# Decode attention on one core: K, V and weights in 8 MB transfers of 64 KB runs, two ring slots at a time

## The chip, the core and the metric

The kernel runs on one core of a Trainium2 chip. The metric is the device time of one execution in microseconds (us); most executions of one kernel agree within 0.3%. All runs told here are of the fast, undisturbed state. A ratio is the mean time of one kernel's fast runs over the mean of the other kernel's fast runs of the same rounds, so it is not quite the ratio of the medians that are quoted.

PE is the matmul engine, VectorE (DVE), ScalarE (ACT) and GpSimd (POOL) are the other compute engines, and SP issues the large DMA transfers. MB in names of transfers means 4,194,304 bytes for "4 MB".

## The reference, cut to what matters

```python
# A: attention of one new token per sequence against a cache; B=4, H=32 heads, Sk=8192, Dh=128, bf16
q = (x @ wq) ...
scores = einsum("bhqd,bhkd->bhqk", q, k_cache) * Dh**-0.5
o = einsum("bhqk,bhkd->bhqd", softmax(scores), v_cache)
a = o @ wo
# B: a gated feed-forward, D=1024, F=3584:  b = x + silu(x@w_gate)*(x@w_up) @ w_down * sigmoid(x@w_r)
return g * a + (1 - g) * b            # g = sigmoid(sum(x * gate_w))
```

K and V are 537 MB together and the weights 39 MB, and each byte is used once. The kernel is therefore a stream: what matters is that the DMA engines never rest.

## The kernel before

A ring of five slots, 32 KB per partition (4 MB) each, holds what has arrived. A "piece" of K or V is two heads, 64 partitions each, so a partition receives one contiguous run of 32 KB. K is transposed on VectorE in four chunks and multiplied on PE; V is multiplied on PE against the probabilities. Eight K pieces make a group, which ends with a softmax over 16 heads. V follows eight pieces behind K.

```python
ring = tile_pool(name="ring", bufs=5)
def slot():
    return ring.tile([P, RING], BF, name="piece", tag="piece")     # 4 MB
...
def k_piece(u):
    ...
    kn = slot()
    nc.sync.dma_start(out=kn[:], in_=kv_view(A_k_cache, u))
    for c in range(JR // CJ):                                      # 4 chunks
        T = ttp.tile([P, CJ, 2, 32, 2], BF, name="T", tag="T")     # two buffers
        nc.vector.transpose(out=T..., in_=kn[:, c * CJ * Dh:(c + 1) * CJ * Dh]...)
        ... 8 matmuls into S_ps
        if c == 0:
            flush()                                                # finish() of the group before
    if t == GT - 1:
        softmax(g)
def softmax(g):
    ... max, all-reduce, exp (ACT) ...
    nc.vector.transpose(out=PT..., in_=PTs[:])
    nc.scalar.copy(out=Bv[0:W, :, :, 0, :], in_=Pv[0:W])
    nc.gpsimd.tensor_copy(out=Bv[W:P, :, :, 1, :], in_=Pv[W:P])
    ... rex (DVE), tot = all-reduce of rex (POOL)
    nc.vector.reciprocal(out=rinv[:], in_=tot[:])
def v_piece(u):
    ...
    nc.sync.dma_start(...)                                         # the last piece in four parts
    ... 32 matmuls into o_ps
    # every fourth piece: evict o_ps
    nc.scalar.activation(out=o_sb[:], in_=o_ps[:, 0, :], func=ACT.Copy, scale=mE[:, 0:1])
    nc.vector.scalar_tensor_tensor(out=o_sb[:], in0=o_ps[:, 1, :], scalar=mE[:, 1:2], in1=o_sb[:], ...)
```

## Time and profile before

| | before |
|---|---|
| median time | 1349.41 us (1349.13 to 1349.46) |
| bytes read | 575.68 MB, 427 GB/s over the span of 1347.8 us |
| PE, VectorE busy | 79%, 47% |
| first to last large packet (packet records) | 1341.5 us |
| from the last large packet to the end | 4.5 us |

The page of the kernel before: engines' busy time, the rate in 40 equal slices of the span, the main DMA queue (packets, MB, share of 16 engines' span), and two groups of transfers (size, and median us from issue to landing).

```profile
PE 1059.3 (79%) x4600; PEld 233.2 (17%) x2412; DVE 631.4 (47%) x375; ACT 41.5 (3%) x46; POOL 47.9 (4%) x115
...
GB/s 403 433 433 422 433 430 430 432 433 430 430 433 430 430 431 434 429 431 432 433 428 432 433 430 430 433 431 429 432 434 429 428 433 434 429 428 434 432 423 323
...
q1 hardware_dynamic: 22104, 575.68, 99.5%
...
piece<-in_A_k_cache_dram SPq DMA_DIRECT2D x64, 4096.0 KB, 39.4
piece<-in_A_v_cache_dram SPq DMA_DIRECT2D x63, 4096.0 KB, 39.1
```

The queue is busy for 99.5% of the span, and between the first and the last slice the rate never falls under 422 GB/s. The last two lines: a transfer lands 39 us after its issue, although 4 MB move in 9.7 us (4.194 MB at 431 GB/s). So about four transfers are queued at most times.

Now the place where compute is slowest, the end of a group (timeline of before: start, duration, engine, line, operation, and in brackets the idle time before and what ended it).

```profile
628.76 0.59 PE L401 MATMUL o_ps<-piece,PB 128*16 128x512 bf16 x2
...
629.40 0.69 ACT L411 ACTIVATE OS<-o_ps,mE 128x512 f32<-128x512 f32 x1 [74.68 <-PE o_ps L401]
630.12 0.75 DVE L412 SCALAR_TENSOR_TENSOR OS<-o_ps,mE,OS 128x512 f32<-128x512 f32 x1 [6.23 <-ACT OS L411]
...
632.48 1.25 DVE L367 STREAM_TRANSPOSE PT<-PTs 128x1024 bf16<-128x1024 bf16 x1 [1.33 <-ACT PTs L365]
...
633.87 1.88 POOL L373 COPY PB<-PT 64x1024 bf16<-64x1024 bf16 x1 [3.86 <-DVE rex L375]
...
636.33 0.25 DVE L379 RECIPROCAL rinv<-tot 128x16 f32<-128x16 f32 x1 [2.48 <-POOL tot L377]
636.50 4.44 DVE L336 STREAM_TRANSPOSE T<-piece 128x2048 uint32<-128x2048 uint32 x2
638.90 3.57 PE L342 MATMUL S_ps<-T,Z 128*128 128x512 bf16 x8 [9.54 <-DVE T L336]
...
647.44 2.31 DVE L336 STREAM_TRANSPOSE T<-piece 128x2048 uint32<-128x2048 uint32 x1 [2.50 <-PE S_ps L342]
```

The scheduler has put the eviction (L412) ahead of the rest of the softmax on VectorE, so everything behind it waits for the V matmuls that end at 629.4 us. The next group's transposes start only at 636.5 us. PE, idle for 9.5 us, then works at half clock (the granted clock is 0.50 from 635 to 645 us): 8 matmuls take 3.57 us, elsewhere 1.90. The first four transposes of the group end at 649.8 us. All this lateness costs nothing: the slices that hold this stretch (the 19th and 20th, each 33.7 us) show 432 and 433 GB/s.

### The profile page before, as it was taken

What the parts mean: (1) busy time and instruction counts of PE and PEld (TensorE: products, weight loads), DVE (VectorE), ACT (ScalarE), POOL (GpSimd) and SP (SyncE); (2) the same over time, 40 slices, a digit from 0 to 9 for tenths busy, and PEclk for the clock granted to TensorE, in tenths of its full rate; (3) what the DMA queues carried; (4) which work ended last, traced back from release to release, by engine and by line L of the source; (5) the groups of instructions that cost most, each with busy time, mean ns of one, the idle gap of its engine ahead of it and who ended that gap; (6) DMA issues with size and microseconds to landing.
All of it is one profiled execution on the core that took longest, in us unless ns stands there. A gap on an engine that the chain in (4) does not pass through costs nothing.

```text
span 1347.8 us, 8253 instructions
## 1 busy us (share of the span) xinstructions
PE 1059.3 (79%) x4600; PEld 233.2 (17%) x2412; DVE 631.4 (47%) x375; ACT 41.5 (3%) x46; POOL 47.9 (4%) x115
## 2 busy tenths in 40 slices
PE   2667779876978868876998769888788859797878
PEld 0111111211111111111212111211112112121111
DVE  3555755535544554454545454444544456346000
ACT  0000010001000010001000010000000010000000
POOL 2000000000000000000000000000000000000000
PEclk8878989898989989989898879899888979999899
DMA  9999999999999999999999999999999999999997
GB/s 403 433 433 422 433 430 430 432 433 430 430 433 430 430 431 434 429 431 432 433 428 432 433 430 430 433 431 429 432 434 429 428 433 434 429 428 434 432 423 323
DMA packets 22162, 576.22 MB, mean 428 GB/s; under 512 B 2399, under 2 KB 2407, under 8 KB 2925
## 3 DMA queue, kind: packets, MB, share of 16 engines
q1 hardware_dynamic: 22104, 575.68, 99.5%
q8 instruction: 27, 0.44, 0.1%
q14 instruction: 11, 0.08, 0.0%
q10 hardware_dynamic: 20, 0.02, 0.0%
HBM read 575.68 MB, written 0.01 MB: 427 GB/s over the span
## 4 chain that ended last, share of the span: by engine, by line
DMA 50%; PE 30%; DVE 11%; issue 6%; ACT 1%; POOL 1%; SPq 0%; DVEq 0%; ACTq 0%
DMA piece<-in_A_k_cache_dram 40%; PE o_ps L401 16%; PE S_ps L342 13%; DVE T L336 10%; DMA piece<-in_A_v_cache_dram 9%; PE small L419 1%; DMA piece<-in_A_wo_dram 1%; POOL PB L373 1%; DVE PT L367 1%; ACT PTs L365 1%; ACT OS L411 1%; DVE OS L412 1%; POOL tot L377 0%; PE acc L188 0%; PE o_ps L225 0%
## 5 line engine op out<-in xcount | busy, mean ns | idle before, releaser
L336 DVE STREAM_TRANSPOSE T<-piece 128x2048 uint32<-128x2048 uint32 x256 | 576.1, 2288 | 437.0 <-DMA piece<-in_A_k_cache_dram 321.1
L342 PE MATMUL S_ps<-T,Z 128*128 128x512 bf16 x2048 | 544.6, 416 | 246.6 <-DVE T L336 235.3
L401 PE MATMUL o_ps<-piece,PB 128*16 128x512 bf16 x2048 | 457.6, 382 | 14.8 <-DMA piece<-in_A_v_cache_dram 14.8
L342 PEld LDWEIGHTS <-Z 128*128 128x128 bf16 x1024 | 108.0, 105 | 667.2 <-issue 664.3
L401 PEld LDWEIGHTS <-PB 128*16 128x16 bf16 x1024 | 91.9, 90 | 373.1 <-issue 361.3
L412 DVE SCALAR_TENSOR_TENSOR OS<-o_ps,mE,OS 128x512 f32<-128x512 f32 x16 | 12.0, 751 | 174.6 <-ACT OS L411 174.6
L326 POOL TENSOR_TENSOR Z<-qa,mq 128x16 bf16<-128x16 bf16 x64 | 16.7, 262 | 1072.3 <-PE S_ps L342 1054.3
L411 ACT ACTIVATE OS<-o_ps,mE 128x512 f32<-128x512 f32 x16 | 11.0, 687 | 1040.5 <-PE o_ps L401 1040.5
L419 PEld LDWEIGHTS small<-selg,OS 128*128 128x128 f32 x128 | 24.9, 273 | 12.2 <-issue 11.1
L419 PE MATMUL small<-selg,OS 128*128 128x8 f32 x128 | 22.3, 302 | 0.0
L353 DVE TENSOR_REDUCE m<-S_ps 128x1 f32<-128x1024 f32 x8 | 9.8, 1225 | 15.9 <-PE S_ps L342 15.9
L188 PE MATMUL acc<-piece,LT 128*4 128x512 bf16 x64 | 14.9, 378 | 1.7 <-DMA piece<-in_A_wo_dram 1.6
L373 POOL COPY PB<-PT 64x1024 bf16<-64x1024 bf16 x8 | 15.1, 1884 | 29.1 <-DVE rex L375 29.1
L372 ACT COPY PB<-PT 64x1024 bf16<-64x1024 bf16 x8 | 15.3, 1908 | 10.6 <-DVE PT L367 10.6
L367 DVE STREAM_TRANSPOSE PT<-PTs 128x1024 bf16<-128x1024 bf16 x8 | 10.0, 1245 | 11.9 <-ACT PTs L365 11.9
L188 PE MATMUL acc<-piece,hT 128*4 128x512 bf16 x56 | 12.4, 379 | 0.0
L131 PE MATMUL small<-identb,x 6*128 6x6 bf16 x8 | 0.6, 194 | 14.2 <-DVE identb L128 14.2
L379 DVE RECIPROCAL rinv<-tot 128x16 f32<-128x16 f32 x8 | 2.0, 253 | 19.9 <-POOL tot L377 19.9
L365 ACT ACTIVATE PTs<-S_ps,negm 128x1024 bf16<-128x1024 f32 x8 | 8.9, 1113 | 70.0 <-DVE negm L362 70.0
L225 PE MATMUL S_ps<-piece,xw 128*4 128x512 bf16 x64 | 6.6, 591 | 3.0 <-DMA piece<-in_A_wq_dram 3.0
L422 DVE SCALAR_TENSOR_TENSOR OT<-small,sgb,rinv 128x8 bf16<-128x8 f32 x16 | 3.2, 202 | 11.7 <-PE small L419 11.7
L358 POOL PARTITION_ALL_REDUCE gmx<-mex x8 | 3.1, 390 | 81.9 <-issue 50.3
(72 smaller groups left out, 74.6 us busy)
## 6 DMA issues: line engine op xcount, KB each, us to landing
piece<-in_A_k_cache_dram SPq DMA_DIRECT2D x64, 4096.0 KB, 39.4
piece<-in_A_v_cache_dram SPq DMA_DIRECT2D x63, 4096.0 KB, 39.1
piece<-in_A_wq_dram SPq DMA_DIRECT2D x2, 4096.0 KB, 22.1
piece<-in_B_w_gate_dram SPq DMA_DIRECT2D x2, 3584.0 KB, 40.1
piece<-in_B_w_up_dram SPq DMA_DIRECT2D x2, 3584.0 KB, 34.6
piece<-in_A_wo_dram SPq DMA_DIRECT2D x6, 1024.0 KB
piece<-in_B_w_down_dram SPq DMA_DIRECT2D x1, 4096.0 KB, 35.6
piece<-in_A_v_cache_dram SPq DMA_DIRECT2D x4, 1024.0 KB, 32.6
```

Source lines behind the costliest of these rows:

```text
L188: nc.tensor.matmul(out_ap, lhsT=lhsT, rhs=rhs, start=start, stop=True, skip_group_check=True)
L326: nc.gpsimd.tensor_tensor(out=Z[:, :, 31:31 + P].rearrange("p e (s d c) -> p e s d c", s=HT, d=QH)[:, :, :, :, 0], in0=qa[:, :, h0:h0 + HT ...
L336: nc.vector.transpose(out=T[:].rearrange("p j h i e -> p (j h i e)").bitcast(U32), in_=kn[:, c * CJ * Dh:(c + 1) * CJ * Dh].bitcast(U32))
L342: nc.tensor.matmul(sps[:, z, :], lhsT=Z[:, he, s:s + P], rhs=T[:, 16 * z:16 * z + 16, half, :, e], start=(t == 0 and c == 0 and he == 0), ...
L365: nc.scalar.activation(out=PTs[:], in_=sps[:].rearrange("p z n -> p (z n)"), func=ACT.Exp, bias=negm[:, 0:1], scale=scale, accum_out=rs[:, ...
L367: nc.vector.transpose(out=PT[:].rearrange("p j i -> p (j i)"), in_=PTs[:])
L372: nc.scalar.copy(out=Bv[0:W, :, :, 0, :], in_=Pv[0:W])
L373: nc.gpsimd.tensor_copy(out=Bv[W:P, :, :, 1, :], in_=Pv[W:P])
L401: nc.tensor.matmul(o_ps[row:row + NM, e, :], lhsT=B_[:, JT * t + c, z, w].rearrange("p e s j -> p (e s j)"), rhs=vn[:, j0 * Dh:(j0 + 4) * ...
L411: nc.scalar.activation(out=o_sb[:], in_=o_ps[:, 0, :], func=ACT.Copy, scale=mE[:, 0:1])
L412: nc.vector.scalar_tensor_tensor(out=o_sb[:], in0=o_ps[:, 1, :], scalar=mE[:, 1:2], in1=o_sb[:], op0=ALU.mult, op1=ALU.add)
L419: nc.tensor.matmul(oT[:, :], lhsT=o_sb[:, q * Dh:(q + 1) * Dh], rhs=selg[:, q].rearrange("p t s -> p (t s)"), start=(q == 0), stop=(q == 3))
```

## The change

The intent is fewer, larger packets. A "pair" is four heads, 32 partitions (one quadrant) each, 8 MB in one transfer, with a contiguous run of 64 KB per partition over two neighbouring slots. With five slots every fifth pair wraps around and comes as two 4 MB transfers. The weights travel the same way, all but `wo`, whose transfers stay at 1 MB and less. A group is now four pairs and has one eviction instead of two.

```diff
-    ring = ctx.enter_context(tc.tile_pool(name="ring", bufs=5))
+    ring = const.tile([P, NS, RING], BF, name="ring")              # NS = 5
+    flat = ring[:].rearrange("p s n -> p (s n)")
+    def load_pair(src, n):
+        a = slots(2)
+        if a + 1 < NS:
+            lo = a * RING
+            nc.sync.dma_start(out=flat[:, lo:lo + 2 * n], in_=src)
+            return [flat[:, lo:lo + n], flat[:, lo + n:lo + 2 * n]]
+        halves = [ring[:, a], ring[:, 0]]
+        for i, half in enumerate(halves):
+            nc.sync.dma_start(out=half[:, 0:n], in_=src[:, i * n:(i + 1) * n])
+        return halves
...
-        return cache[b, h0:h0 + HT].rearrange("h (r j) d -> (h r) (j d)", j=JR)
+        return cache[b, h0:h0 + NQ].rearrange("h (r j) d -> (h r) (j d)", j=2 * JR)
...
-        nc.scalar.copy(out=Bv[0:W, :, :, 0, :], in_=Pv[0:W])
-        nc.gpsimd.tensor_copy(out=Bv[W:P, :, :, 1, :], in_=Pv[W:P])
+        for q in range(NQ):                       # quadrants 0, 2 on ACT; 1, 3 on POOL
+            ...
...
-        cut = 4 if u == NT - 1 else 1
+        if d < ND - 1:
+            vs = load_pair(vv, RING)
+        else:                                     # the last pair: 4 MB, then 4 x 1 MB
+            ...
```

More of the change, by code (lines that the diff above doesn't have):

```diff
@@ L69 @@
     DT = D // P
-    HT = 2
-    JR = Sk * HT // P
-    JC = JR // 16
-    GT = 8
-    JT = JC // 2
-    RT = 4
-    GH = GT * HT
-    RH = RT * HT
     NQ = 4
-    QH = NQ // HT
+    QP = P // NQ
+    JR = Sk // QP // 2
     CJ = 32
-    NT = Bn * H // HT
-    LAG = GT
+    JT = JR // CJ
+    RD = 2 * JT
+    GD = QP // RD
+    GH = GD * NQ
+    ND = Bn * H // NQ
+    LAG = GD
     FR = 4
@@ L87 @@
     RING = JR * Dh
+    NS = 5
     assert Sq == 1 and Dh == P and D % P == 0 and F % (P * FR) == 0
-    assert H == 32 and JR == 128 and JT * GT == 32 and GT % RT == 0 and H % GH == 0 and D % NB == 0
+    assert H % GH == 0 and JR == 128 and RD * GD == QP and D % NB == 0
     scale = float(Dh) ** -0.5
@@ L103, with slots @@
     nc.at_finalize(keep_weights)
+    ring = const.tile([P, NS, RING], BF, name="ring")
+    turn = [0]
+    def slots(n):
+        at = turn[0]
+        turn[0] = (at + n) % NS
+        return at
+    flat = ring[:].rearrange("p s n -> p (s n)")
[9 more added lines that the diff above has]
+        return halves
     def small(shape, dtype=F32):
         return mps.tile(shape, dtype, name="small", tag="small")
-    def slot():
-        return ring.tile([P, RING], BF, name="piece", tag="piece")
     NX = Bn + 2
@@ L134 @@
     xT = [xw[:, t, 0:Bn] for t in range(DT)]
-    R = const.tile([P, 4, P], BF)
+    R = ptp.tile([P, 4, P], BF, name="R", tag="PTs")
     nc.gpsimd.memset(R[:], 0.0)
@@ L140, with band @@
                                 base=-(64 * half + e), pattern=[[0, 4], [-2, 32]], channel_multiplier=1)
-    m32 = const.tile([P, GT, NQ], F32)
-    nc.gpsimd.memset(m32[:], 1.0)
-    nc.gpsimd.affine_select(out=m32[:], in_=m32[:], compare_op=ALU.is_ge, fill=0.0,
-                            base=0, pattern=[[-JT, GT], [-32, NQ]], channel_multiplier=1)
-    nc.gpsimd.affine_select(out=m32[:], in_=m32[:], compare_op=ALU.is_ge, fill=0.0,
-                            base=JT - 1, pattern=[[JT, GT], [32, NQ]], channel_multiplier=-1)
-    mask8 = const.tile([P, GH], F32)
-    nc.vector.tensor_reduce(out=mask8[:], in_=m32[:].rearrange("p t (s q) -> p (t s) q", q=QH), axis=AX.X, op=ALU.add)
-    pen8 = const.tile([P, GH], F32)
-    nc.vector.tensor_scalar(out=pen8[:], in0=mask8[:], scalar1=-1.0, scalar2=3.0e38, op0=ALU.add, op1=ALU.mult)
-    nmask8 = const.tile([P, GH], F32)
-    nc.vector.tensor_scalar(out=nmask8[:], in0=mask8[:], scalar1=-scale, scalar2=None, op0=ALU.mult)
-    selg = const.tile([P, 4, RT, HT], F32)
+    def band(t, width, steps):
+        nc.gpsimd.memset(t[:], 1.0)
+        nc.gpsimd.affine_select(out=t[:], in_=t[:], compare_op=ALU.is_ge, fill=0.0, base=0,
+                                pattern=[[-s, n] for s, n in steps], channel_multiplier=1)
+        nc.gpsimd.affine_select(out=t[:], in_=t[:], compare_op=ALU.is_ge, fill=0.0, base=width - 1,
+                                pattern=[[s, n] for s, n in steps], channel_multiplier=-1)
+    mask3 = const.tile([P, GD, NQ], F32)
+    band(mask3, RD, [(RD, GD), (QP, NQ)])
+    mask = mask3[:].rearrange("p t q -> p (t q)")
+    pen = const.tile([P, GH], F32)
+    nc.vector.tensor_scalar(out=pen[:], in0=mask, scalar1=-1.0, scalar2=3.0e38, op0=ALU.add, op1=ALU.mult)
+    nmask = const.tile([P, GH], F32)
+    nc.vector.tensor_scalar(out=nmask[:], in0=mask, scalar1=-scale, scalar2=None, op0=ALU.mult)
+    selg = const.tile([P, 4, GD, NQ], F32)
     nc.gpsimd.memset(selg[:], 0.0)
@@ L156 @@
         nc.gpsimd.affine_select(out=selg[:], in_=selg[:], compare_op=ALU.not_equal, fill=1.0,
-                                base=-8 * e, pattern=[[-1, 4], [-32, RT], [-4, HT]], channel_multiplier=1)
+                                base=-16 * e, pattern=[[-1, 4], [-32, GD], [-4, NQ]], channel_multiplier=1)
     mE4 = const.tile([P, 2, 4], F32)
-    nc.gpsimd.memset(mE4[:], 1.0)
-    nc.gpsimd.affine_select(out=mE4[:], in_=mE4[:], compare_op=ALU.is_ge, fill=0.0,
-                            base=0, pattern=[[-8, 2], [-32, 4]], channel_multiplier=1)
-    nc.gpsimd.affine_select(out=mE4[:], in_=mE4[:], compare_op=ALU.is_ge, fill=0.0,
-                            base=7, pattern=[[8, 2], [32, 4]], channel_multiplier=-1)
+    band(mE4, 16, [(16, 2), (32, 4)])
     mE = const.tile([P, 2], F32)
@@ L166 @@
     mq = const.tile([P, 1, NQ], BF)
-    nc.gpsimd.memset(mq[:], 1.0)
-    nc.gpsimd.affine_select(out=mq[:], in_=mq[:], compare_op=ALU.is_ge, fill=0.0,
-                            base=0, pattern=[[0, 1], [-32, NQ]], channel_multiplier=1)
-    nc.gpsimd.affine_select(out=mq[:], in_=mq[:], compare_op=ALU.is_ge, fill=0.0,
-                            base=31, pattern=[[0, 1], [32, NQ]], channel_multiplier=-1)
-    ZW = 31 + P + 1
+    band(mq, QP, [(0, 1), (QP, NQ)])
+    ZW = QP - 1 + P + 1
     Zt = [const.tile([P, 4, ZW], BF, name=f"Z{i}") for i in range(2)]
-    PB = [const.tile([P, 32, 2, 2, 2, HT, 4], BF, name=f"PB{i}") for i in range(2)]
+    PB = [const.tile([P, QP, 2, 2, 2, NQ, 4], BF, name=f"PB{i}") for i in range(2)]
     for z in Zt + PB:
@@ L209, in add_x, with x_rows, wq_piece @@
             mm_acc(acc[:, n * NB:(n + 1) * NB], dg[:], xf[:, n * NB:(n + 1) * NB])
-    wqv = A_wq.rearrange("(c t) n -> c t n", t=DT)
-    wgv = B_w_gate.rearrange("(c t) f -> c t f", t=DT)
-    wuv = B_w_up.rearrange("(c t) f -> c t f", t=DT)
-    wdv = B_w_down.rearrange("(g f r) n -> f g r n", f=P, r=FR)
+    TW = DT // 2
+    wdv = B_w_down.rearrange("(f i) n -> f (i n)", f=P)
     wov = A_wo.rearrange("(g p r) n -> p g r n", p=P, r=FR)
-    TW = 4
-    def x_rows(ps, w, t0, nb):
-        for t in range(TW):
-            for k in range(4):
-                for z in range((nb - k + 3) // 4):
-                    i = 4 * z + k
-                    nc.tensor.matmul(ps[32 * k:32 * k + Bn, z, :], lhsT=xT[t0 + t], rhs=w[:, t, i * NB:(i + 1) * NB],
-                                     start=(t0 + t == 0), stop=(t0 + t == DT - 1), skip_group_check=True)
-    def wq_piece(t0):
-        w = slot()[:, :TW * H * Dh].rearrange("p (t n) -> p t n", t=TW)
-        nc.sync.dma_start(out=w, in_=wqv[:, t0:t0 + TW, :])
-        x_rows(q_ps, w, t0, H * Dh // NB)
+    def x_rows(ps, ws, nb, cols):
+        for half, w in enumerate(ws):
+            for t in range(TW):
+                for k in range(4):
+                    for z in range((nb - k + 3) // 4):
+                        nc.tensor.matmul(ps[32 * k:32 * k + Bn, z, :], lhsT=xT[TW * half + t], rhs=cols(w, t, 4 * z + k),
+                                         start=(half + t == 0), stop=(half == 1 and t == TW - 1), skip_group_check=True)
+    def wq_piece():
+        N = H * Dh
+        ws = load_pair(A_wq.rearrange("(c t) n -> c (t n)", t=DT), TW * N)
+        x_rows(q_ps, ws, N // NB, lambda w, t, i: w[:, t * N + i * NB:t * N + (i + 1) * NB])
     def q_done():
@@ L246, in q_done, with gu_piece, cols @@
         nc.vector.tensor_copy(out=qa[:].rearrange("p e h b -> p e (h b)"), in_=qa_ps[:])
-    def gu_piece(view, w_i, t0):
-        w = slot()[:, :TW * F].rearrange("p (t n) -> p t n", t=TW)
-        nc.sync.dma_start(out=w, in_=view[:, t0:t0 + TW, :])
-        x_rows((o_ps, acc4)[w_i], w, t0, FG)
+    def gu_piece(view, w_i):
+        ws = load_pair(view.rearrange("(c t) f -> c (t f)", t=DT), TW * F)
+        def cols(w, t, i):
+            row = w[:, t * F:(t + 1) * F].rearrange("p (f i r) -> p f i r", i=FG, r=FR)
+            return row[:, :, i, :]
+        x_rows((o_ps, acc4)[w_i], ws, FG, cols)
     def h_done():
@@ L264, in h_done, with wd_piece @@
                                         in1=c12[:, 1:2, :].to_broadcast([P, kn, Bn]), op=ALU.mult)
-    def wd_piece(g0, ng):
-        w = slot()[:, :ng * FR * D].rearrange("p (g r n) -> p g r n", g=ng, r=FR)
-        nc.sync.dma_start(out=w.rearrange("p g r n -> p g (r n)"),
-                          in_=wdv[:, g0:g0 + ng].rearrange("f g r n -> f g (r n)"))
-        for g in range(ng):
-            for r in range(FR):
-                for n in range(NH):
-                    mm_acc(acc[:, n * NB:(n + 1) * NB], hT[:, g0 + g, r, :], w[:, g, r, n * NB:(n + 1) * NB],
-                           start=(g0 + g + r == 0))
+    def wd_piece():
+        NR = FG * FR // 2
+        ws = load_pair(wdv, NR * D)
+        for i in range(FG * FR):
+            w = ws[i // NR]
+            for n in range(NH):
+                at = (i % NR) * D + n * NB
+                mm_acc(acc[:, n * NB:(n + 1) * NB], hT[:, i // FR, i % FR, :], w[:, at:at + NB], start=(i == 0))
     WB = P * FR // Dh
@@ L294, in wo_block @@
         if home not in wo_home:
-            wo_home[home] = slot().rearrange("p (g r n) -> p g r n", g=4, r=FR)
+            wo_home[home] = ring[:, slots(1)].rearrange("p (g r n) -> p g r n", g=4, r=FR)
         w = wo_home[home][:, at]
@@ L313, in flush, with heads, kv_view, k_pair @@
             pending.pop(0)()
-    def heads(u):
-        return divmod(u * HT, H)
-    def kv_view(cache, u):
-        b, h0 = heads(u)
-        return cache[b, h0:h0 + HT].rearrange("h (r j) d -> (h r) (j d)", j=JR)
-    def k_piece(u):
-        b, h0 = heads(u)
-        g, t = divmod(u, GT)
-        Z = Zt[u % 2]
-        nc.gpsimd.tensor_tensor(out=Z[:, :, 31:31 + P].rearrange("p e (s d c) -> p e s d c", s=HT, d=QH)[:, :, :, :, 0],
-                                in0=qa[:, :, h0:h0 + HT, b:b + 1].to_broadcast([P, 4, HT, QH]),
-                                in1=mq[:].rearrange("p o (s d) -> p o s d", s=HT).to_broadcast([P, 4, HT, QH]), op=ALU.mult)
+    def heads(d):
+        return divmod(d * NQ, H)
+    def kv_view(cache, d):
+        b, h0 = heads(d)
+        return cache[b, h0:h0 + NQ].rearrange("h (r j) d -> (h r) (j d)", j=2 * JR)
+    def k_pair(d):
+        b, h0 = heads(d)
+        g, t = divmod(d, GD)
+        Z = Zt[d % 2]
+        nc.gpsimd.tensor_tensor(out=Z[:, :, QP - 1:QP - 1 + P].rearrange("p e (q c) -> p e q c", c=QP)[:, :, :, 0],
+                                in0=qa[:, :, h0:h0 + NQ, b], in1=mq[:].to_broadcast([P, 4, NQ]), op=ALU.mult)
         if t == 0:
@@ L331, in k_piece @@
         sps = S_ps[g]
-        kn = slot()
-        nc.sync.dma_start(out=kn[:], in_=kv_view(A_k_cache, u))
-        for c in range(JR // CJ):
+        ks = load_pair(kv_view(A_k_cache, d), RING)
+        for n in range(RD):
+            kn, c = ks[n // JT], n % JT
             T = ttp.tile([P, CJ, 2, 32, 2], BF, name="T", tag="T")
@@ L337, in k_piece @@
                                 in_=kn[:, c * CJ * Dh:(c + 1) * CJ * Dh].bitcast(U32))
-            s = 31 - (JT * t + c)
+            s = QP - 1 - (RD * t + n)
             for he in range(4):
@@ L342, in k_piece @@
                     nc.tensor.matmul(sps[:, z, :], lhsT=Z[:, he, s:s + P], rhs=T[:, 16 * z:16 * z + 16, half, :, e],
-                                     start=(t == 0 and c == 0 and he == 0),
-                                     stop=(t == GT - 1 and c == JT - 1 and he == 3))
-            if c == 0:
+                                     start=(t == 0 and n == 0 and he == 0),
+                                     stop=(t == GD - 1 and n == RD - 1 and he == 3))
+            if n == 0:
                 flush()
-        if t == GT - 1:
+        if t == GD - 1:
             softmax(g)
@@ L354, in softmax @@
         mex = stat.tile([P, GH], F32, tag="mex")
-        nc.vector.scalar_tensor_tensor(out=mex[:], in0=mask8[:], scalar=m1[:, 0:1], in1=pen8[:],
+        nc.vector.scalar_tensor_tensor(out=mex[:], in0=mask, scalar=m1[:, 0:1], in1=pen[:],
                                        op0=ALU.mult, op1=ALU.add)
@@ L359, in softmax @@
         gmm = stat.tile([P, GH], F32, tag="gmm")
-        nc.vector.tensor_tensor(out=gmm[:], in0=gmx[:], in1=nmask8[:], op=ALU.mult)
+        nc.vector.tensor_tensor(out=gmm[:], in0=gmx[:], in1=nmask[:], op=ALU.mult)
         negm = stat.tile([P, 1], F32, tag="negm")
         nc.vector.tensor_reduce(out=negm[:], in_=gmm[:], axis=AX.X, op=ALU.add)
-        PTs = ptp.tile([P, 1024], BF, name="PTs")
+        PTs = ptp.tile([P, 1024], BF, name="PTs", tag="PTs")
         rs = stat.tile([P, 1], F32, tag="rs")
@@ L368, in softmax @@
         B_ = PB[g % 2]
-        W = P // HT
         Pv = PT[:].rearrange("p (q j) i -> p i q j", j=4)
         Bv = B_[:].rearrange("p i z w e s j -> p i (z w e) s j")
-        nc.scalar.copy(out=Bv[0:W, :, :, 0, :], in_=Pv[0:W])
-        nc.gpsimd.tensor_copy(out=Bv[W:P, :, :, 1, :], in_=Pv[W:P])
+        for q in range(NQ):
+            at = slice(QP * q, QP * (q + 1))
+            if q % 2 == 0:
+                nc.scalar.copy(out=Bv[at, :, :, q, :], in_=Pv[at])
+            else:
+                nc.gpsimd.tensor_copy(out=Bv[at, :, :, q, :], in_=Pv[at])
         rex = stat.tile([P, GH], F32, tag="rex")
-        nc.vector.tensor_scalar(out=rex[:], in0=mask8[:], scalar1=rs[:, 0:1], scalar2=None, op0=ALU.mult)
+        nc.vector.tensor_scalar(out=rex[:], in0=mask, scalar1=rs[:, 0:1], scalar2=None, op0=ALU.mult)
         tot = stat.tile([P, GH], F32, tag="tot")
@@ L380, in softmax, with v_pair @@
         rinv_t[g] = rinv
-    NM = 8 * HT
-    def v_piece(u):
-        b, h0 = heads(u)
-        g, t = divmod(u, GT)
-        row = 32 * (t % RT)
-        B_ = PB[g % 2]
-        vn = slot()
-        vv = kv_view(A_v_cache, u)
-        cut = 4 if u == NT - 1 else 1
-        for c in range(cut):
-            lo, hi = c * RING // cut, (c + 1) * RING // cut
-            nc.sync.dma_start(out=vn[:, lo:hi], in_=vv[:, lo:hi])
+    NM = 8 * NQ
+    def v_pair(d):
+        b, h0 = heads(d)
+        g, t = divmod(d, GD)
+        row = NM * t
+        B_ = PB[g % 2]
+        vv = kv_view(A_v_cache, d)
+        if d < ND - 1:
+            vs = load_pair(vv, RING)
+        else:
+            vs = [ring[:, slots(1)] for _ in range(2)]
+            nc.sync.dma_start(out=vs[0], in_=vv[:, 0:RING])
+            for c in range(4):
+                lo, hi = c * RING // 4, (c + 1) * RING // 4
+                nc.sync.dma_start(out=vs[1][:, lo:hi], in_=vv[:, RING + lo:RING + hi])
         n = 0
-        for c in range(JT):
+        for c in range(RD):
+            vn = vs[c // JT]
             for z in range(2):
@@ L399, in v_piece @@
                     for e in range(2):
-                        j0 = 32 * c + 16 * z + 8 * w + 4 * e
+                        j0 = CJ * (c % JT) + 16 * z + 8 * w + 4 * e
                         nc.tensor.matmul(o_ps[row:row + NM, e, :],
-                                         lhsT=B_[:, JT * t + c, z, w].rearrange("p e s j -> p (e s j)"),
-                                         rhs=vn[:, j0 * Dh:(j0 + 4) * Dh], start=(n == 0), stop=(n == JR // 8 - 1),
+                                         lhsT=B_[:, RD * t + c, z, w].rearrange("p e s j -> p (e s j)"),
+                                         rhs=vn[:, j0 * Dh:(j0 + 4) * Dh], start=(n == 0), stop=(n == 4 * RD - 1),
                                          skip_group_check=True)
@@ L407, in v_piece @@
                         flush()
-        if t % RT < RT - 1:
+        if t < GD - 1:
             return
@@ L413, in v_piece @@
                                        op0=ALU.mult, op1=ALU.add)
-        r0 = RH * (t // RT)
         def finish():
-            oT = small([P, RH])
+            oT = small([P, GH])
             for q in range(4):
@@ L420, in finish @@
                                  rhs=selg[:, q].rearrange("p t s -> p (t s)"), start=(q == 0), stop=(q == 3))
-            hg = h0 + HT - RH
-            nc.vector.scalar_tensor_tensor(out=OT[:, hg:hg + RH, b], in0=oT[:, :], scalar=sgb[:, 1, b:b + 1],
-                                           in1=rinv_t[g][:, r0:r0 + RH], op0=ALU.mult, op1=ALU.mult)
+            hg = h0 + NQ - GH
+            nc.vector.scalar_tensor_tensor(out=OT[:, hg:hg + GH, b], in0=oT[:, :], scalar=sgb[:, 1, b:b + 1],
+                                           in1=rinv_t[g][:], op0=ALU.mult, op1=ALU.mult)
         pending.append(finish)
     gates()
-    wq_piece(0)
-    wq_piece(TW)
+    wq_piece()
     q_done()
-    side = [lambda: gu_piece(wgv, 0, 0), lambda: gu_piece(wgv, 0, TW), lambda: gu_piece(wuv, 1, 0),
-            lambda: (gu_piece(wuv, 1, TW), h_done()), lambda: wd_piece(0, 4), lambda: wd_piece(4, FG - 4)]
-    GE = NWB - RH // WB
+    gu_piece(B_w_gate, 0)
+    side = {1: lambda: (gu_piece(B_w_up, 1), h_done()), GD - 1: wd_piece}
+    GE = NWB - GH // WB
     order = []
-    for u in range(NT - 2):
-        order += [("k", u)] + [("v", u - LAG)] * (u >= LAG)
-    order += [("k", NT - 2), ("k", NT - 1)] + [("v", u) for u in range(NT - 2 - LAG, NT)]
-    for kind, u in order:
+    for d in range(ND):
+        order += [("k", d)] + [("v", d - LAG)] * (d >= LAG)
+    order += [("v", d) for d in range(ND - LAG, ND)]
+    for kind, d in order:
         if kind == "k":
-            k_piece(u)
-        if (kind, u) == ("v", NT - 1):
+            k_pair(d)
+            if d in side:
+                side[d]()
+        if (kind, d) == ("v", ND - 1):
             for g in range(2):
@@ L444 @@
         if kind == "v":
-            v_piece(u)
-        if side and (kind == "v" or u < LAG):
-            side.pop(0)()
-        if (kind, u) == ("k", NT // 2):
+            v_pair(d)
+        if (kind, d) == ("k", ND // 2):
             add_x()
-        if (kind, u) == ("v", NT - RT):
+        if (kind, d) == ("v", ND - 2):
             o_rows(0, GE)
@@ L459 @@
         use()
-    res = const.tile([Bn, D], BF)
+    res = ttp.tile([Bn, D], BF, name="res", tag="T")
     nc.vector.tensor_copy(out=res[:, 0:NB], in_=acc[:, 0:NB])
```

## The prediction

> **What bounds the kernel now.** The DMA engines. The queue table gives 575.68 MB and a busy share of 99.5% of the 16 engines; the stretch view gives 431 GB/s from 100 to 600 us and from 700 to 1260 us. By the packet records, the engines stand idle for about 5 us in all, nearly all in the first and last microseconds. No compute engine is near full: PE 79%, DVE 47% (page, part 1). The longest DVE wait (321 us) is for K data, so removing compute waits buys nothing. The Trainium skill ("DMA: Bandwidth & Descriptors", "Where 436 GB/s comes from") puts the fabric ceiling at 435.2 GB/s; this trace agrees, its best slice is 434. At the ceiling 575.68 MB take 1323 us, so faster by 2% (under 1322.4 us) is out of reach.
>
> **What the change saves.** Median packet times are 160 ns for 4 KB, 312 for 8 KB, 1062 for 28 KB, 1215 for 32 KB: a line of about 11 ns plus bytes at 27.2 B/ns. A 64 KB packet should then take about 2419 ns against 2 x 1215. Four fifths of 16,384 K/V packets pair up: 6,550 x 11 ns / 16 = 4.5 us. Down weights in 28 KB instead of 8 KB packets: 0.5 us. About 55 transfers fewer, one 9 ns semaphore packet each on every engine: 0.5 us. Sum, an estimate: 5.5 us (0.4%), all on the critical path. Matmuls, transposes and bytes stay the same.
>
> **What it adds.** Coarser hand-over. Before, four 4 MB pieces are queued (39 us from issue to landing). After, of five slots two are consumed, two are in flight and one is spare; a pair may issue only when the first half of the pair two back is consumed. In the steady state that is 9.5 us after landing for K (four transposes of 2.29 us), some 9 us after for V, against 19.4 us of transfer in flight: about 9 us of margin. At each group's end it nearly vanishes. The DVE order puts the softmax chain after the eviction, which waits for a V pair's 64 matmuls (14.1 us); transposes start 7.1 us after that in the trace before, and now some 1.9 us later, because two GpSimd copies of 1.9 us precede the total that the reciprocal waits for. PE then restarts at half clock (about 10 us there before). A hand schedule with these durations and 1.0 us from issue to first packet gives 0 to 20 us of DMA gaps in total over seven boundaries and the start; my middle is about 4 us.
>
> **Prediction.** 1349.4 - 5.5 + about 3 to 4: 1347 us, 80% range 1341 to 1362. Chances: faster by over 2% 0.01, same 0.94, slower by over 2% 0.05.
>
> **What would show each step.** Right: some 12,000 packets on the main queue; 64 KB packets near 2419 ns; slices of 433 GB/s where undisturbed; dips in the slices once per group (about every 155 us), with the DMA queue's waits ended by DVE transposes or PE output matmuls just before a gap. If there are no dips, the time is about 1344.
>
> **What would make it wrong.** 64 KB runs split into smaller packets (no gain); partitions 64 KB apart reading slower from HBM (the query weights already have that pitch: median 1213 ns); PE at half clock much longer, now that it idles in longer blocks: 20 to 40 us more.

The 1323 us in it are an estimate from that page's ceiling of 435.2 GB/s; no run here measures the ceiling itself.

## More of the kernel before

At the very end PE waits for the last weights. The timeline of before:

```profile
1342.57 1.02 PE L188 MATMUL acc<-piece,LT 128*4 128x512 bf16 x4 [0.17 <-DMA piece<-in_A_wo_dram]
1343.81 1.02 PE L188 MATMUL acc<-piece,LT 128*4 128x512 bf16 x4 [0.22 <-DMA piece<-in_A_wo_dram]
```

DMA ends last, and only four matmuls and the output follow.

## The result, and the profile after

The changed kernel takes 1357.45 us (median; 1357.18 to 1359.34) against 1349.41, a ratio of 1.0063 (95% interval 1.0048 to 1.0077): 0.6% slower, within the predicted range, but on the other side of the kernel before. The middle of the prediction, 1347, missed by 10.5 us. The time lies in the range because the range was 21 us wide, not because the sum was right. All outputs are right.

The page after:

```profile
PE 1041.7 (77%) x4536; PEld 228.8 (17%) x2348; DVE 621.4 (46%) x358; ACT 51.3 (4%) x46; POOL 57.1 (4%) x91
...
GB/s 410 428 434 432 433 434 425 441 436 420 426 432 426 440 427 434 432 432 430 403 430 433 434 425 426 432 425 442 412 420 441 436 421 404 430 423 442 432 420 301
...
q1 hardware_dynamic: 13688, 575.68, 98.8%
```

PE and VectorE have a little less work; ScalarE and GpSimd have about 10 us more each, at 4% of the span. There are 8,416 packets fewer, but the queue is busy for a smaller share of a longer span, and slices of 403, 412 and 404 GB/s have appeared. (Slices above 435 are presumably an effect of counting whole 64 KB packets in one slice.)

The same group end in the timeline after:

```profile
635.70 0.59 PE L411 MATMUL o_ps<-ring,PB 128*32 128x512 bf16 x2
636.33 0.69 ACT L421 ACTIVATE OS<-o_ps,mE 128x512 f32<-128x512 f32 x1 [154.93 <-PE o_ps L411]
637.05 0.75 DVE L422 SCALAR_TENSOR_TENSOR OS<-o_ps,mE,OS 128x512 f32<-128x512 f32 x1 [13.14 <-ACT OS L421]
...
639.42 1.25 DVE L370 STREAM_TRANSPOSE PT<-PTs 128x1024 bf16<-128x1024 bf16 x1 [1.33 <-ACT PTs L368]
...
640.80 3.80 POOL L379 COPY PB<-PT 32x1024 bf16<-32x1024 bf16 x2 [9.96 <-DVE rex L381]
...
645.18 0.25 DVE L385 RECIPROCAL rinv<-tot 128x16 f32<-128x16 f32 x1 [4.40 <-POOL tot L383]
645.35 4.44 DVE L339 STREAM_TRANSPOSE T<-ring 128x2048 uint32<-128x2048 uint32 x2
647.75 3.57 PE L345 MATMUL S_ps<-T,Z 128*128 128x512 bf16 x8 [11.46 <-DVE T L339]
...
656.23 4.51 DVE L339 STREAM_TRANSPOSE T<-ring 128x2048 uint32<-128x2048 uint32 x2 [2.43 <-PE S_ps L345]
658.57 0.33 SPq L109 DMA_DIRECT2D ring<-in_A_k_cache_dram  x1
```

The chain is almost the same as before, 1.9 us longer where VectorE's reciprocal waits for two GpSimd copies. The difference is the last line: the next K pair can be issued only now, when the fourth transpose has freed a slot. By the packet records the transfer in flight ran out on one engine after another, on most by 657.4 us and on the last at 659.4, and the next packets begin at 659.5 us. Those 16 first packets take 3.06 to 3.52 us, where an undisturbed one takes 2.42. In this run clear dry stretches stand at three of the seven group ends (657 to 660, 971 to 972 and 1128 to 1131 us; 2.1, 0.4 and 2.0 us averaged over the engines), and slow first packets at these and a fourth (337 to 348 us), 3.1 us in all by the same average. Windows of five microseconds of the kernel after show the first hole (busy time per engine, then PE's granted clock, DMA share, GB/s):

```profile
650.00:655.00 5.00, 5.00 (x18) 2.40 (x12) 2.45 (x2) 0.00 (x0) 0.00 (x0) 0.50 1.09 472
655.00:660.00 5.00, 4.33 (x18) 0.82 (x8) 3.77 (x2) 0.00 (x0) 0.00 (x0) 0.90 0.76 262
660.00:665.00 5.00, 4.28 (x19) 0.87 (x9) 5.00 (x3) 0.00 (x0) 0.00 (x0) 1.00 0.48 210
```

The end of the kernel after, in its timeline:

```profile
1307.86 14.82 PE L411 MATMUL o_ps<-ring,PB 128*32 128x512 bf16 x60 [5.38 <-DMA ring<-in_A_v_cache_dram]
...
1340.40 0.69 ACT L421 ACTIVATE OS<-o_ps,mE 128x512 f32<-128x512 f32 x1 [74.19 <-PE o_ps L411]
...
1345.33 7.07 PE L192 MATMUL acc<-ring,LT 128*4 128x512 bf16 x32 [0.36 <-DVE LT L291]
1352.22 0.68 DVE L469 CAST res<-acc 4x512 bf16<-4x512 f32 x1 [6.95 <-PE acc L192]
```

PE sat idle for 5.38 us until the whole of the last V pair but one had landed, then had two pairs to do and is late from there on. The last packet lands at 1347.0 us (1.8 + 1345.2, table below), but PE's last 32 matmuls end at 1352.4 us. Before, the end waited for DMA; now it waits for PE.

Where the 7.6 us of the two profiled runs lie (packet records; "busy" is the sum of all packet times of the main queue over 16 engines):

| us | before | after | after − before |
|---|---|---|---|
| start to first large packet | 1.8 | 1.8 | 0.0 |
| first to last large packet | 1341.5 | 1345.2 | +3.7 |
| last large packet to end | 4.5 | 8.5 | +4.0 |
| busy | 1340.9 | 1339.2 | −1.7 |

The changed kernel moves its bytes with slightly less packet time, yet takes longer in the middle, and longer again at the end.

### The profile page after: what moved, and what is told of

Same layout as the page of the kernel before. It is cut to its first block, busy times and chain, and to the rows that moved or that the text cites. A ratio compares the mean times of both kernels' runs of the same rounds, so it can differ in the third digit from the quotient of the medians.

```text
span 1355.5 us, 7979 instructions
## 1 busy us (share of the span) xinstructions
PE 1041.7 (77%) x4536; PEld 228.8 (17%) x2348; DVE 621.4 (46%) x358; ACT 51.3 (4%) x46; POOL 57.1 (4%) x91
## 3 DMA queue, kind: packets, MB, share of 16 engines
q1 hardware_dynamic: 13688, 575.68, 98.8%
## 4 chain that ended last, share of the span: by engine, by line
DMA 44%; PE 28%; issue 13%; DVE 11%; POOL 1%; ACT 1%; another core or an unknown queue 0%; DVEq 0%; SPq 0%; ACTq 0%
DMA ring<-in_A_k_cache_dram 37%; PE o_ps L411 16%; PE S_ps L345 10%; DVE T L339 10%; DMA ring<-in_A_v_cache_dram 5%; DMA ring<-in_B_w_gate_dram 3%; PE acc L192 1%; POOL PB L379 1%; PE small L428 1%; DVE PT L370 1%; ACT PTs L368 1%; DVE OS L422 0%; ACT OS L421 0%; POOL tot L383 0%
## 5 line engine op out<-in xcount | busy, mean ns | idle before, releaser
L339 DVE STREAM_TRANSPOSE T<-ring 128x2048 uint32<-128x2048 uint32 x256 | 569.7, 2280 | 457.3 <-DMA ring<-in_A_k_cache_dram 384.1
L345 PE MATMUL S_ps<-T,Z 128*128 128x512 bf16 x2048 | 529.1, 405 | 239.9 <-DVE T L339 239.5
L411 PE MATMUL o_ps<-ring,PB 128*32 128x512 bf16 x2048 | 460.3, 386 | 35.7 <-DMA ring<-in_A_v_cache_dram 35.6
L411 PEld LDWEIGHTS <-PB 128*32 128x32 bf16 x1024 | 100.5, 98 | 391.8 <-issue 374.1
L379 POOL COPY PB<-PT 32x1024 bf16<-32x1024 bf16 x16 | 30.1, 1879 | 55.4 <-DVE rex L381 55.0
L377 ACT COPY PB<-PT 32x1024 bf16<-32x1024 bf16 x16 | 30.5, 1906 | 10.7 <-DVE PT L370 10.6
L192 PE MATMUL acc<-ring,LT 128*4 128x512 bf16 x64 | 14.5, 379 | 0.7 <-DVE LT L291 0.7
L428 PEld LDWEIGHTS small<-selg,OS 128*128 128x128 f32 x64 | 12.9, 283 | 7.6 <-issue 5.4
L428 PE MATMUL small<-selg,OS 128*128 128x16 f32 x64 | 11.7, 321 | 0.9 <-DVE OS L422 0.9
L192 PE MATMUL acc<-ring,hT 128*4 128x512 bf16 x56 | 12.2, 379 | 0.0
```

Source lines behind the costliest of these rows:

```text
L192: nc.tensor.matmul(out_ap, lhsT=lhsT, rhs=rhs, start=start, stop=True, skip_group_check=True)
L339: nc.vector.transpose(out=T[:].rearrange("p j h i e -> p (j h i e)").bitcast(U32), in_=kn[:, c * CJ * Dh:(c + 1) * CJ * Dh].bitcast(U32))
L345: nc.tensor.matmul(sps[:, z, :], lhsT=Z[:, he, s:s + P], rhs=T[:, 16 * z:16 * z + 16, half, :, e], start=(t == 0 and n == 0 and he == 0), ...
L377: nc.scalar.copy(out=Bv[at, :, :, q, :], in_=Pv[at])
L379: nc.gpsimd.tensor_copy(out=Bv[at, :, :, q, :], in_=Pv[at])
L411: nc.tensor.matmul(o_ps[row:row + NM, e, :], lhsT=B_[:, RD * t + c, z, w].rearrange("p e s j -> p (e s j)"), rhs=vn[:, j0 * Dh:(j0 + 4) * ...
```

## The experiments

Theory A, mine: the coarser hand-over costs twice, in DMA queues that run dry at group ends, and in a tail where PE starts late on a pair that lands as a whole; the packet saving is real. Rival B: 64 KB runs in 8 MB transfers move bytes no faster, or more slowly. Rival C: the new layout (quarter copies, one head per quadrant) makes the compute chain slower, whatever the transfers. Rival D: the saving comes from fewer transfers, not from longer runs. The kernel before had a median of 1349.39 to 1349.43 us in all three sets of runs, so sets can be compared. The changed kernel itself was timed in the first set alone (four runs), so every difference from it is one between sets.

### e1_tail: the last V pair but one as two halves

```diff
-        if a + 1 < NS:
+        if a + 1 < NS and not split:
-            vs = load_pair(vv, RING)
+            vs = load_pair(vv, RING, split=(d == ND - 2))
```

> The changed kernel, but the last V pair but one arrives as two 4 MB transfers. Theory A (the loss is hand-over: gaps at group boundaries, plus a tail where PE waits 5.4 us for a whole 8 MB pair that lands late): the PE wait before that pair goes, the time after the last weight packet falls from 8.5 to about 4.5 us, total 1357.4 - 4 = 1353 to 1354.5 us. Rival B (the 64 KB form of transfer itself moves bytes more slowly) and rival C (the new layout, one head per quadrant, slows the softmax chain) expect no change: 1357 us.

Measured: 1353.79 us (1351.21 to 1355.60), 3.7 us less than the changed kernel. In the profiled run 4.6 us follow the last large packet, no longer 8.5. The 5.4 us wait before that pair is gone; what PE still waits for is the last pair:

```profile
1324.79 13.11 PE L411 MATMUL o_ps<-ring,PB 128*32 128x512 bf16 x60 [2.06 <-DMA ring<-in_A_v_cache_dram]
...
1343.73 7.07 PE L192 MATMUL acc<-ring,LT 128*4 128x512 bf16 x32 [0.35 <-DVE LT L291]
```

The tail is a loss of its own of about 4 us, and one 8 MB transfer makes it. The profiled run was the slowest of the five: its queue ran dry at four group ends, and first to last packet took 1347.4 us, 2.2 more than in the kernel after. So the loss at group ends varies from run to run.

### e2_halves: the new layout, all pairs in halves

```diff
-        if a + 1 < NS:
+        if False:
-        halves = [ring[:, a], ring[:, 0]]
+        halves = [ring[:, a], ring[:, (a + 1) % NS]]
```

> The changed kernel with its new layout, but every pair (K, V, weights) arrives as two 4 MB transfers of 32 KB runs, each with its own completion and its own slot. A: gaps and tail go, the packet saving goes too: 1348 to 1350.5 us, as before the change; DMA idle under 5.5 us inside the run. C: the layout still costs, 1354 us or more. B: also about 1349.

Measured: 1350.87 us (1349.10 to 1351.93), ratio to before 1.0007 (0.9994 to 1.0019). The profiled run (1349.14 us) has no dry queue. This is 0.4 us over the range A gave, and the spread is larger than that. The interval includes no difference from before; its upper end is 2.6 us. The run is less clean than its edit, though. Its timeline at the same group end shows that the scheduler ordered the work differently:

```profile
620.26 1.11 ACT L368 ACTIVATE PTs<-S_ps,negm 128x1024 bf16<-128x1024 f32 x1 [147.28 <-DVE negm L365]
...
620.73 7.07 PE L411 MATMUL o_ps<-ring,PB 128*32 128x512 bf16 x32 [1.18 <-DMA ring<-in_A_v_cache_dram]
```

The exponentials come before the last V matmuls, so the softmax no longer stands behind the eviction. Against rival C the run is therefore weak; e8_slow_before, below, is the better test.

### e3_evict: the softmax no longer behind the eviction

ScalarE alone evicts, into two bf16 buffers, with a scale that is written after the exponentials. That dependence keeps the scheduler from placing the eviction ahead of them. Transfers are untouched.

```diff
+        mE_t[g] = stat.tile([P, 2], F32, name="mEg", tag="mE")
+        nc.vector.scalar_tensor_tensor(out=mE_t[g][:], in0=mE[:], scalar=rs[:, 0:1], in1=mE[:], op0=ALU.max, op1=ALU.min)
-        nc.scalar.activation(out=o_sb[:], in_=o_ps[:, 0, :], func=ACT.Copy, scale=mE[:, 0:1])
-        nc.vector.scalar_tensor_tensor(out=o_sb[:], in0=o_ps[:, 1, :], scalar=mE[:, 1:2], in1=o_sb[:], ...)
+        me = mE_t.get(g + 1, mE)
+        for e in range(2):
+            nc.scalar.activation(out=o_sb[:, e], in_=o_ps[:, e, :], func=ACT.Copy, scale=me[:, e:e + 1])
```

> The changed kernel with its transfers as they are, but the eviction of the outputs is done by ACT alone into two bf16 buffers and made to depend on the exponentials, so the softmax chain no longer stands behind the V pair's matmuls. A: K transposes of a new group start at landing instead of 7 us late, no drained DMA queue at group boundaries, no first packets of 3.1 to 3.5 us there: 1350 to 1352.5 us, tail unchanged. B: unchanged at 1357. C: only in part faster (1355 or more), since the quarter copies remain.

Measured: 1350.18 us (1349.26 to 1350.52), 7.3 us less than the changed kernel. The timeline of e3_evict at the same group end:

```profile
638.91 4.44 DVE L340 STREAM_TRANSPOSE T<-ring 128x2048 uint32<-128x2048 uint32 x2
641.31 3.57 PE L346 MATMUL S_ps<-T,Z 128*128 128x512 bf16 x8 [5.57 <-DVE T L340]
...
649.60 0.33 SPq L109 DMA_DIRECT2D ring<-in_A_k_cache_dram  x1
```

The issue comes 9 us earlier, and the packet records show no dry queue between the start and the last microseconds. First to last packet shrinks from 1345.2 to 1338.1 us: 7.1 us were lost at the boundaries (3.8 us less packet time and 3.3 us less idle time, averaged over the engines). Without that loss the stretch is 3.4 us shorter than in the kernel before. This falls against B and C: the transfers and the layout are those of the changed kernel, quarter copies included. The tail stays (7.5 us), as it should.

### e5_both: e1 and e3 together, and the total ahead of the copies

```diff
+ the edits of e1_tail, e3_evict and e4_total (below), nothing else
```

> e1 and e3 together, and the row-sum total ahead of the GpSimd copies. A: both losses gone, the packet saving of about 5 us stays: 1344 to 1348 us, 0.1 to 0.4% faster than the kernel before the change. B: no better than 1349. C: about 1351.

Measured: 1346.65 us (1345.66 to 1347.96), ratio to before 0.998 (0.9967 to 0.9992), so faster than the kernel before by 0.2%, and than the changed kernel by 0.8%. The gains of e1 and e3 add up: 3.7 + 7.3 = 11.0 us expected from the parts, 10.8 measured; the edit of e4, also in here, had no dry queue left to remove. The end waits for DMA again in its timeline:

```profile
1340.47 1.02 PE L192 MATMUL acc<-ring,LT 128*4 128x512 bf16 x4 [0.22 <-DMA ring<-in_A_wo_dram]
```

### e4_total: only the row-sum total ahead of the GpSimd copies

```diff
+        ... rex, tot, rinv: moved from after the copies to before the transpose of PT
         PT = ptp.tile([P, 32, 32], BF, name="PT")
```

> The changed kernel, with the row-sum total issued on GpSimd before its two 1.9 us copies, so the reciprocal no longer makes VectorE wait 4.4 us ahead of the next transposes. Theory A (each us of lateness at a group boundary eats the margin of the next pair's issue): chain shorter by about 4 us at each boundary, most drains go, 1352 to 1354.5 us; tail unchanged. Rival C (the lateness there doesn't matter, only the eviction's form did in the run before): 1357 us.

Measured: 1351.72 us (1351.44 to 1353.14), 5.7 us less than the changed kernel and slightly better than A's range. At the same group end the transposes start 4.6 us after V's last matmul, no longer 9.1, and the issue follows:

```profile
640.51 4.44 DVE L339 STREAM_TRANSPOSE T<-ring 128x2048 uint32<-128x2048 uint32 x2
...
653.80 0.33 SPq L109 DMA_DIRECT2D ring<-in_A_k_cache_dram  x1
```

No dry queue is left in the packet records, although the eviction still stands in the chain.

### e6_warm: PE kept busy across the boundary

```diff
+        if d < ND - 1:
+            wps = small([P, 512])
+            for _ in range(50):
+                nc.tensor.matmul(wps[:, :], lhsT=identb[:], rhs=PB[g % 2]..., start=True, stop=True, ...)
```

> The changed kernel, with 50 idle matmuls (10.7 us, result unused) on PE after each group's last V pair, so PE doesn't rest before the next group's K pair. A: the granted clock stays 1.0 there, the third and fourth transposes come about 4 us sooner, so drains mostly go: 1352 to 1355 us. If the clock plays no part in the drains: 1357 us or slower.

Measured: 1351.62 us (1350.93 to 1352.62), 5.8 us less, by adding useless work. Windows of e6_warm (the clock is the third number from the end):

```profile
645.00:650.00 5.00, 4.40 (x25) 1.45 (x13) 4.33 (x2) 0.00 (x0) 0.00 (x0) 1.00 1.01 433
650.00:655.00 5.00, 3.91 (x18) 0.83 (x9) 4.98 (x4) 0.00 (x0) 0.00 (x0) 1.00 0.99 419
```

The clock is 1.00 where it was 0.50 in the kernel after, and no dry queue is left at the group ends. The Trainium skill ("TensorE: Matmul & The Clock Gate", Part 1) says that PE falls to half clock after an idle window of about 3.4 us. This trace agrees: 11.5 us of idle were followed by 8 matmuls in 3.57 us, elsewhere 1.90; in e3_evict 5.6 us of idle were enough. No run here tests the 3.4 us.

Each of three edits (e3, e4, e6) alone removes most of the boundary loss (7.3, 5.7 and 5.8 us). The timelines show why. For the six group ends with a V pair, the table has the time from V's last matmul to the issue of the next K pair, and the ends at which the packet records show a dry queue (more than half of the engines without a packet):

| run | last V matmul to K issue, us | dry at |
|---|---|---|
| kernel after | 20.1, 17.3, 22.3, 19.9, 20.4, 22.1 | 22.3, 20.4, 22.1 |
| e1_tail | 22.4, 14.0, 22.3, 20.0, 20.4, 20.2 | 22.4, 22.3, 20.4, 20.2 |
| e6_warm | 18.3, 17.6, 18.9, 18.3, 18.3, 18.3 | none |
| e4_total | 17.8, 14.0, 17.9, 17.8, 15.0, 17.9 | none |
| e3_evict | 14.9, 14.9, 13.9, 14.9, 14.0, 14.9 | none |
| e7_slow_after (below) | 27.6, 17.2, 25.3, 27.8, 25.2, 27.8 | all but 17.2 (and at the first group end, which has no V pair) |

At these group ends the queue ran dry wherever the issue came more than 20.1 us after V's last matmul, and nowhere else. The changed kernel stands right at that edge. Of its 19.9 to 22.3 us, 1.9 come from the second GpSimd copy, which the new layout brought. So rival C is right in one thing, that the layout lengthens the chain; without these 1.9 us only two ends would have come later than 20.1 us, by 0.3 us at most (an estimate from the table). No run has the 8 MB transfers without that copy, so how the 7.3 us divide between the two is open.

### e7_slow_after and e8_slow_before: the same extra chain in both kernels

```diff
-        nc.vector.transpose(out=PT..., in_=PTs[:])
+        for _ in range(9):
+            nc.vector.transpose(out=PT..., in_=PTs[:])
```

> The changed kernel with 8 more probability transposes (1.245 us each, same result) in each softmax, which lengthens the VectorE chain at each of seven boundaries by about 5.3 us net. A: no margin is left there, so the DMA queue drains longer at each: 1375 to 1395 us. Rival (the loss is not made by hand-over at the boundaries): under 1360 us.

> The kernel before the change with the same 8 more transposes in each softmax (about 7 us net, 10 us of VectorE). A: four queued pieces (39 us) hide it: 1349 to 1352 us, no drain. Rival: slower by as much as the changed kernel with the same edit.

Measured: 1386.52 us (1386.34 to 1386.74) for the changed kernel with the edit, 29 us more; 1349.40 us (1349.20 to 1349.52) for the kernel before with it, no change. The rates by slice, first e7_slow_after:

```profile
GB/s 408 439 426 428 440 404 415 436 442 419 351 423 426 451 424 428 436 432 432 364 426 428 432 429 352 425 436 439 339 436 439 427 434 323 442 421 437 442 415 300
```

and e8_slow_before:

```profile
GB/s 404 432 431 425 431 430 429 434 429 433 429 435 427 432 431 434 429 431 431 430 432 431 432 428 433 433 428 431 433 433 425 433 433 432 427 431 434 431 423 326
```

In five slices the changed kernel falls to 323 to 364 GB/s; six dry stretches of about 2 to 7.6 us (idle time averaged over 16 engines) stand in its packet records. The finer hand-over of the kernel before hides its delay wholly.

The same edit did not make the same delay, though, because the scheduler mixed the extra transposes among those of K. By the timelines, the K issue of the changed kernel came 3 to 8 us later at six of the seven group ends, 35 us in all (at the first end, without V, counted from the exponentials), of which 29 passed into the time: about four fifths, on an engine that is "not critical". In the kernel before, the fourth transpose of the next group came only 1.5 to 4.0 us later where a V piece precedes it. That is 21.7 to 22.6 us after V's last matmul, as late as at the worst group ends of the changed kernel (22.3), and it cost nothing. So a late chain alone, rival C, does not make the loss; it takes the coarse hand-over as well. The two kernels also differ in layout; the edit was not run on e2_halves.

### e9_run32: 8 MB transfers again, but 32 KB runs

```diff
+    PAD = 32                                                       # 64 bytes between slots
+    rpad = const.tile([P, NS, RING + PAD], BF, name="ring")
-            nc.sync.dma_start(out=flat[:, lo:lo + 2 * n], in_=src)
+            nc.sync.dma_start(out=rpad[:, a:a + 2, 0:n], in_=src.rearrange("p (s n) -> p s n", s=2))
```

(applied to e5_both)

> The fastest variant so far (e5_both: 1346.65 us), its transfers still 8 MB, but 64 bytes of padding between ring slots, so each run is 32 KB (28 KB for weights) instead of 64 KB. Theory A (the saving comes from fewer packets, about 11 ns each): DMA busy time up by about 4.5 us, 1350 to 1352 us. Rival D (the saving comes from fewer, larger transfers, whatever the run): 1346 to 1347.5 us.

Measured: 1347.96 us (1347.69 to 1348.02), ratio to before 0.9988 (0.9974 to 1.0002), 1.3 us more than e5_both, where A had 3.4 to 5.4 us. Packet time did rise, from 1335.9 to 1339.0 us, but the time followed by less than half. D's range was missed too, by 0.5 us. So run length is worth about 1.3 us here. e10_flush, which behaves as e5_both and ran in the same rounds as e9_run32, confirms it: 1.4 us less, with no overlap of the ranges. The remaining 1.45 us between e9_run32 and the kernel before (an interval that just includes none) come from something else in the new form (fewer transfers, the down weights in 28 KB rows, the end), which these runs do not separate.

### e10_flush: the group's output matmuls later in the next K pair

> e5_both with the output-transposing matmuls of the group before moved from behind the first chunk to behind the seventh chunk of the next K pair. A: no drain is left in e5_both for it to remove, so the same within 0.1%: 1345.5 to 1348 us.

```diff
-            if n == 0:
+            if n == RD - 2:
                 flush()
```

Measured: 1346.58 us (1345.49 to 1346.96), ratio to before 0.9977 (0.9965 to 0.9990), the same as e5_both, as expected: no dry queue was left to remove.

## Why the prediction was right or wrong, point by point

- **"What bounds the kernel now": right.** Every difference of the profiled runs lies in packet time, DMA idle time or the tail. e8_slow_before added some 80 us of VectorE work (8 transposes x 1.245 us x 8 groups) at no cost.
- **Where the dips would be: right in kind.** The issue before the hole at 657 us follows a VectorE transpose directly. But not every group ends in a hole, as the prediction had it: three did in the profiled run, four in that of e1_tail.
- **A 64 KB packet near 2419 ns: right.** The median is 2418 ns over 6,656 packets, which are not split. The forecast of "some 12,000 packets" fits too: the page's 13,688 contain 1,524 semaphore packets of 4 bytes, and 12,164 carry data.
- **"Sum, an estimate: 5.5 us, all on the critical path": too large.** Without dry queues (e5_both) packet time falls by 5.0 us (1340.9 to 1335.9), but the stretch from first to last packet by 3.3 us (1341.5 to 1338.2), and the measured time by 2.8 us. The sum was right in packet time and wrong in treating it as elapsed time. The packet records account for the difference. The time by which packets overlap one another (more than 16 under way, averaged over 16 engines) also fell, from 3.5 to 2.3 us, and the semaphore packets, which run beside the others, fell by 0.5 us of packet time. Both were in the packet time and never in the elapsed time.
- **"At each group's end it nearly vanishes": right, with its causes.** The eviction (e3_evict), the GpSimd copies (e4_total) and the half clock (e6_warm) each showed as a cause. The size was too low: the middle was "about 4 us", the loss was 7.1 us in the profiled runs and 7.3 us in the medians. One missing part is measured: after a dry queue the first packet on each engine takes 0.6 to 1.1 us more than the usual 2.42, where the prediction had only 1.0 us from issue to first packet; in the profiled run this comes to some 3.1 us of the 7.1.
- **The step that failed: the sum "1349.4 - 5.5 + about 3 to 4" has no term for the end of the kernel.** The tail cost 4.0 us (8.5 against 4.5 us after the last packet), and e1_tail gave 3.7 of it back. The prediction asked only whether the DMA queue would run dry; it did not ask what PE still has to do when the last large transfer lands. It is not the whole miss of 10.5 us: the saving was 2.8 instead of 5.5, the boundaries cost 7.3 instead of 3 to 4, and the tail 3.7 instead of nothing, three misses of about the same size and all to the same side.
- **What would make it wrong:** none of the three came about. 64 KB runs were not split, they were not slower, and PE's mean granted clock was 0.904 (0.914 before).

Put together from the corrected terms: 1349.4 − 2.8 + 7.3 + 3.7 = 1357.6 us, against 1357.45 measured. The first term stands in e5_both, the others are the differences of medians of e3_evict and e1_tail, so this is a check that they add, not a new result.

## What to carry to other kernels

When a stream already keeps the DMA engines busy, enlarging its transfers has little packet overhead left to win (0.2% here, in e5_both), while each doubling halves the number of hand-overs: count the margin, in microseconds of queued transfer, at the slowest place of the loop, not in its steady state. Delay on an engine that is off the critical path is free until that margin is gone, and then passes into the time for the most part; the same edit cost 0 us with four transfers queued and 29 us with one or two. Keep the last transfers small, so that the work after the final landing stays short.

## What the Trainium skill lacked or had wrong

- "DMA: Bandwidth & Descriptors", "Where 436 GB/s comes from": the fabric ceiling of 435.2 GB/s agrees with the best slice of the kernel before, 434 GB/s. The page's measured table, for transfers issued from GpSimd, ends with 425 GB/s at 16 MB; here a queue of 4 MB transfers issued from SP held 431 GB/s for 500 us, so the table is not the limit for a full queue.
- Same page, "Rules for kernel authors": "≥1 MiB per DMA" for bandwidth is a lower bound only. The page lacks the other side, what a size costs when little is queued behind it: 8 MB transfers with too little queued behind them lost 7.3 us at group ends and 3.7 us in the tail.
- Same page: what it says of the cost per packet is for small transfers and small descriptors; it gives none for long runs. Here medians were 160 ns for 4 KB, 312 for 8 KB, 1215 for 32 KB and 2418 for 64 KB, about 11 ns beyond the bytes for each; in time, 64 KB instead of 32 KB runs were worth 1.3 us of 1347 (e5_both against e9_run32).
- No page says that the first packets after a dry queue take longer: here 16 of 3.06 to 3.52 us instead of 2.42 us, after a queue that was empty for about 2 us.
- "TensorE: Matmul & The Clock Gate", Part 1: agrees (half clock after 11.5 us idle). It lacks that the clock can matter through another engine: half clock held back VectorE's double-buffered transposes, and with them a DMA issue; keeping PE busy with 50 unused matmuls won 5.8 us (e6_warm), though the first transposes started as late as before (9.1 us after V's last matmul in both).
